# A first product that streams 512 columns instead of 448 in the half-size block products

## The chip, the cores and the metric

One NeuronCore of a Trainium2 chip runs the whole kernel. The metric is the device time of one execution in microseconds (us); several runs are taken and their median is compared. One execution is also recorded by the hardware profiler, and all rows below come from that record.

## The reference

The reference is attention followed by two feed-forward blocks, all in float32.

```
scores = cap * tanh(scale * q @ k.T / cap)          # 2 batches x 12 heads, 448 x 448, head size 64
x = softmax(scores) @ v  -> (896 tokens, 768)
x = x / sqrt(mean(x*x) + 1e-6) * rms_g              # first block
x = (silu(x @ w_gate) * (x @ w_val)) @ w_out        # 768 -> 1536 -> 768
h = x @ w_in                                        # second block, 768 -> 2048
out = (max(h, 0) + alpha * min(h, 0)) @ w_out       # 2048 -> 768
```

## The kernel before, in words

Tokens lie along the free dimension: each of the two batches has S = 448 tokens, so every large matmul streams 448 columns. A float32 number is split into a high part and a low part of the type fp32r, and a product of two such numbers is made from three matmuls: high by high, low by high and high by low.

The program has four stretches after attention, written out by hand in one order for all engines (`manual_schedule`). Stretch g is the first layer of the first block, o its second layer, z the first layer of the second block, f its second layer. The first layers g and z multiply 2 x 2 blocks in a scheme with seven half-size products (P1 to P7) instead of eight; the sums and differences that this takes are made by VectorE (`tt`, L564), and weights are combined on GpSimd (L115). The second layers o and f are plain sums over the inner dimension (L657, L659 and L661).

One half-size product is `product` (L373): for each of two rows r (two halves `ps[:, r, :]` of a PSUM pair of banks) nine matmuls (L380) add into the same 448 columns: three inner blocks k (K3 = 3) times the three high/low pairs. So a product is 18 matmuls, and each has its own weights, which TensorE loads ahead of it (LDWEIGHTS, PEld in the profile). A bank holds 512 columns, of which 448 are used; every reader takes `[:, :, :S]`. The moving operand `xh` is a tile of 128 x 3 x 448, so its three blocks k lie behind each other.

`slots` is the list of products in program order. `pslot` (L613) makes a slot of g or z; around the slots, `do` hangs the work of the other engines (weight splitting `w_hi` L120 and `w_lo` L124, evacuations L515 and L564, activations L894 and L897). The weight units come by DMA (L93), three at a time. TensorE runs the slots in the written order; a matmul waits when its weights' split (ScalarE, VectorE), its operand or its PSUM bank is not ready.

`pslot` calls `product` for 62 slots: 34 in g and 28 in z. Four more products of g stand outside it (the calls in the prologue, before 128 us), and P5 and P6 of the first two groups of g go through another function (`products`, L385).

Of the kernel before, what the change touches and what calls it, by code (L numbers as in the profile page):

```python
# [18 lines left out]
B, H, S, D = 2, 12, 448, 64  # L19
# [17 lines left out]
K3 = KD // 2  # L37
# [17 lines left out]
def attn_moe_kernel(ctx: ExitStack, tc: tile.TileContext, units, qk_in, v, sel, w, gvec, alpha, cap, out):  # L55
# [314 lines left out]

    fill_ps = {}

    def product(ps, u, name, first, rows=(0, 1)):  # L373

        wh, wl = h_t[u], l_t[u]
        xh, xl = oper[name]
        for r in rows:
            mm = [(a[:, r * K3 + k, :], x[:, k, :]) for a, x in ((wh, xh), (wl, xh), (wh, xl)) for k in range(K3)]
            for n, (lhs, rhs) in enumerate(mm):
                nc.tensor.matmul(  # L380
                    ps[:, r, :S], lhs, rhs, start=first and n == 0, stop=n == len(mm) - 1,
                    skip_group_check=True,
                )

    def products(pss, us, name):  # L385

        xh, xl = oper[name]
        both = [(ps, u) for ps, u in zip(pss, us)]
        mm = [(p, x, k, m) for k in range(K3) for p, x in ((h_t, xh), (l_t, xh)) for m in both]
        mm += [(h_t, xl, k, m) for m in both for k in range(K3)]  # L390
        for n, (wt, x, k, (ps, u)) in enumerate(mm):
            for r in range(2):
                nc.tensor.matmul(  # L393
                    ps[:, r, :S], wt[u][:, r * K3 + k, :], x[:, k, :], start=n < len(both),
                    stop=x is xl and k == K3 - 1, skip_group_check=True,
                )


    with tc.manual_schedule():
# [25 lines left out]
        r = raw.pop(0)  # L425
# [95 lines left out]
        norm_now(last)  # L521
        late = []
        product(pa[0], ("g", 0, "A11"), "B11", True, rows=(0,))
        norm(last - 1, "u")
        square(last - 1)
        product(pa[0], ("g", 0, "A11"), "B11", True, rows=(1,))
        for m in range(NP - 3, NP):
            xnorm(m, late)
# [6 lines left out]
        sum4("g", 1)  # L535
        rms_tail(B - 1)
        product(pa[1], ("g", 1, "A11"), "B11", True)
        first_sum(1, ct("c21"))
        w_hi(("g", 1, "S1"))
# [13 lines left out]
        def psum():  # L553
            turn[0] += 1
            return pair_tile(*pools[(turn[0] - 1) % 4])
# [55 lines left out]
        BANK = {"P1": pa, "P2": pa, "P6": pb, "P7": pb, "P4": pb, "P5": pc, "P3": pc}  # L611

        def pslot(lay, p, g):  # L613

            first = p in ("P1", "P6", "P5")
            wn, xn = OPER[p]

            def pe():
                if first:
                    BANK[p][g] = psum()  # L620
                if lay == "g" and p in ("P5", "P6") and g < 2:
                    if g == 1:
                        products([BANK[p][0], BANK[p][1]], [("g", i, wn) for i in range(2)], xn)
                    return
                product(BANK[p][g], (lay, g, wn), xn, first)

            at_of[lay, g, p] = len(slots)
            slots.append((pe, (lay, g, wn)))
# [409 lines left out]
```

## Time and profile before

| | us |
|---|---|
| median of 3 runs | 587.43 |
| the three runs | 584.61, 587.43, 587.48 |
| the profiled execution, its own time | 588.38 |
| the profiled execution, span from first to last instruction | 586.6 |

The stretches of the profiled execution, by the lines of TensorE: attention and the prologue to 143.5 us, products of g by `pslot` from 143.5 to 270.6 (612 matmuls), o to 359.9 (432), z to 465.4 (504), f to the end (576). In the rows, a matmul's own duration (some 367 ns) is longer than the time from one start to the next (some 205 ns), since matmuls are pipelined; the time from start to start is what counts here and is called the gap.

### The profile page before, as it was taken

The numbers are of one execution on the slowest core, as the hardware profiler recorded it, in microseconds if no ns is written. First come the engines' busy times: TensorE is split into PE (matmuls) and PEld (weight loads), VectorE is DVE, ScalarE is ACT, GpSimd is POOL, SyncE is SP. The second block draws the span as 40 slices with busy tenths as digits, with TensorE's granted clock in tenths as the row PEclk, the third lists the DMA queues.
The fourth block names the chain that finished last, engine by engine and source line by source line (L and its number), as shares of the span: only waits on it lengthen the run. The fifth ranks groups of instructions, "written<-read, shape, count | busy, mean of one in ns | idle before, by whom it ended". The sixth has DMA issues, their size and how long they took to land.

```text
span 586.6 us, 7330 instructions
## 1 busy us (share of the span) xinstructions
PE 576.8 (98%) x2939; PEld 475.1 (81%) x2939; DVE 391.8 (67%) x425; ACT 342.4 (58%) x393; POOL 111.1 (19%) x60
## 2 busy tenths in 40 slices
PE   8999999999999999999999999999899999999997
PEld 5444434598899999999999999999899989999996
DVE  5557997999997577669642563879976977613100
ACT  6999979668454453465724344577765986332101
POOL 0002873110056144110000072402441000000000
PEclk9999999999999999999999999999999999999999
DMA  8655420310234444023651633005421435431002
GB/s 272 210 195 168 132 76 20 117 46 1 95 122 161 117 152 162 7 101 108 215 162 57 237 137 108 0 1 162 139 78 57 138 129 162 161 149 55 0 1 94
DMA packets 16650, 66.05 MB, mean 113 GB/s; under 512 B 3560, under 2 KB 4200, under 8 KB 16616
## 3 DMA queue, kind: packets, MB, share of 16 engines
q1 hardware_dynamic: 16040, 65.07, 33.3%
q8 instruction: 23, 0.38, 0.3%
q10 hardware_dynamic: 432, 0.38, 0.2%
q0 software_dynamic: 144, 0.13, 0.1%
q14 instruction: 11, 0.09, 0.0%
HBM read 62.66 MB, written 2.75 MB: 112 GB/s over the span
## 4 chain that ended last, share of the span: by engine, by line
PE 81%; DVE 9%; ACT 5%; issue 2%; DMA 2%; SPq 0%; ACTq 0%; DVEq 0%
PE s L380 19%; PE m L380 14%; PE m L661 6%; PE m L659 6%; PE m L657 6%; PE oo L212 5%; PE s L659 5%; PE s L661 5%; PE s L657 5%; PE s L189 4%; DVE b L564 2%; PE us L228 2%; DVE wt L107 2%; PE m L393 1%; DVE wl L124 1%
## 5 line engine op out<-in xcount | busy, mean ns | idle before, releaser
L124 DVE TENSOR_TENSOR wl<-wt,wh 128x768 fp32r<-128x768 f32 x98 | 105.9, 1088 | 93.3 <-ACT wh L120 93.0
L115 POOL TENSOR_TENSOR wt<-wt 128x768 f32<-128x768 f32 x40 | 91.5, 2295 | 260.3 <-DVE wt L107 146.4
L120 ACT CAST wh<-wt 128x768 fp32r<-128x768 f32 x98 | 81.4, 835 | 87.3 <-PE m L659 37.2
L103 ACT CAST top<-raw 128x768 f16<-128x768 bf16 x68 | 72.6, 1075 | 47.3 <-DVE wt L107 39.3
L107 DVE SCALAR_TENSOR_TENSOR wt<-raw,top 128x768 uint32<-128x768 uint32 x68 | 69.5, 1025 | 3.5 <-ACT top L103 3.4
L380 PE MATMUL s<-xh,wh 128*128 128x448 f32 x222 | 58.2, 370 | 0.0
L380 PE MATMUL s<-xl,wh 128*128 128x448 f32 x222 | 57.7, 368 | 0.0
L380 PE MATMUL s<-xh,wl 128*128 128x448 f32 x222 | 57.7, 368 | 0.0
L661 PE MATMUL m<-ks,wl 128*128 128x448 f32 x176 | 51.6, 367 | 0.0
L657 PE MATMUL m<-ks,wh 128*128 128x448 f32 x176 | 51.6, 367 | 0.0
L380 PE MATMUL m<-xh,wh 128*128 128x448 f32 x174 | 45.5, 369 | 1.8 <-ACT b L515 1.5
L661 PE MATMUL s<-ks,wl 128*128 128x448 f32 x160 | 47.0, 366 | 0.0
L657 PE MATMUL s<-ks,wh 128*128 128x448 f32 x160 | 46.9, 366 | 0.0
L380 PEld LDWEIGHTS s<-xh,wh 128*128 128x128 f32 x222 | 41.5, 188 | 5.5 <-issue 0.9
L199 ACT ACTIVATE pt<-s,cinv 128x896 f32<-128x896 f32 (+1 forms) x48 | 41.3, 908 | 7.6 <-PE s L189 7.4
L659 PE MATMUL m<-b,wh 128*128 128x448 f32 x156 | 45.6, 367 | 0.0
L380 PE MATMUL m<-xh,wl 128*128 128x448 f32 x174 | 45.2, 368 | 0.0
L380 PE MATMUL m<-xl,wh 128*128 128x448 f32 x174 | 45.2, 367 | 0.0
L380 PEld LDWEIGHTS s<-xl,wh 128*128 128x128 f32 x222 | 41.7, 188 | 4.1
L380 PEld LDWEIGHTS s<-xh,wl 128*128 128x128 f32 x222 | 41.7, 188 | 4.0
L212 PE MATMUL oo<-pt,vt 128*64 128x448 f32 x192 | 41.3, 551 | 1.0 <-ACT pt L201 1.0
L201 ACT ACTIVATE pt<-pt,cap_t 128x1792 f32<-128x1792 f32 (+1 forms) x24 | 38.6, 1607 | 0.8
(143 smaller groups left out, 909.8 us busy)
## 6 DMA issues: line engine op xcount, KB each, us to landing
raw<-w_in SPq DMA_DIRECT2D x68, 768.0 KB
rw<-qk_in SPq DMA_DIRECT2D x11, 480.0 KB
vt<-v_in SPq DMA_DIRECT2D x12, 256.0 KB
out<-o SPq DMA_DIRECT2D x5, 448.0 KB
gt<-us SPq DMA_DIRECT2D x22, 3.5 KB
rw<-qk_in ACTq DMA_DIRECT2D x1, 256.0 KB
rw<-qk_in SPq DMA_DIRECT2D x1, 224.0 KB
out<-o SPq DMA_DIRECT2D x1, 224.0 KB
```

The lines of the kernel that those rows point to most:

```text
L103: nc.scalar.copy(top_of[u].bitcast(F16)[:, 1::2], raw_t[u].bitcast(BF16)[:, 4:4 * UW + 4:4])
L107: nc.vector.scalar_tensor_tensor(out=f_t[u].bitcast(U32), in0=raw_t.pop(u).bitcast(U32)[:, 1:2 * UW + 1:2], scalar=13, in1=top_of.pop(u), ...
L115: nc.gpsimd.tensor_tensor(out=t, in0=f_t[a], in1=f_t[b], op=op)
L120: nc.scalar.copy(h_t[u], f_t[u].rearrange("p (k m) -> p k m", m=P))
L124: nc.vector.tensor_tensor(out=l_t[u], in0=f_t[u].rearrange("p (k m) -> p k m", m=P), in1=h_t[u], op=ALU.subtract)
L199: nc.scalar.activation(out=t[:, n:n + w], in_=st.pop((i, g))[:, :w, :S], func=AF.Tanh, scale=cinv)
L201: nc.scalar.activation(out=t[:, :n], in_=t[:, :n], func=AF.Exp, scale=cap_t)
L212: nc.tensor.matmul(oo[i][h * D:h * D + D, :S], vv[:, 2 * c + h, :], t[:, n, :], start=c == 0, stop=c == 3, skip_group_check=True,)
L380: nc.tensor.matmul(ps[:, r, :S], lhs, rhs, start=first and n == 0, stop=n == len(mm) - 1, skip_group_check=True,)
L657: nc.tensor.matmul(dst[l], wh[:, o, :], xh[l], start=first, stop=False)
L659: nc.tensor.matmul(dst[l], wh[:, o, :], xl[l], start=False, stop=False)
L661: nc.tensor.matmul(dst[l], wl[:, o, :], xh[l], start=False, stop=fin)
```

## The change

`product` gets a flag `wide`, which `pslot` sets. With it the first matmul of row 0 (high by high, k = 0) streams 512 columns of the flattened operand: the 448 of block k = 0 and the first 64 of block k = 1. Its output is 512 columns of the bank, of which columns 448 to 511 are read by nobody. All other matmuls are as before.

```
-    def product(ps, u, name, first, rows=(0, 1)):
+    def product(ps, u, name, first, rows=(0, 1), wide=False):
         wh, wl = h_t[u], l_t[u]
         xh, xl = oper[name]
         for r in rows:
             mm = [(a[:, r * K3 + k, :], x[:, k, :]) for a, x in ((wh, xh), (wl, xh), (wh, xl)) for k in range(K3)]
+            if wide and r == 0:
+                mm[0] = wh[:, r * K3, :], xh.rearrange("p k s -> p (k s)")[:, :512]
             for n, (lhs, rhs) in enumerate(mm):
                 nc.tensor.matmul(
-                    ps[:, r, :S], lhs, rhs, start=first and n == 0, stop=n == len(mm) - 1,
+                    ps[:, r, :rhs.shape[-1]], lhs, rhs, start=first and n == 0, stop=n == len(mm) - 1,
                     skip_group_check=True,
                 )
...
-                product(BANK[p][g], (lay, g, wn), xn, first)
+                product(BANK[p][g], (lay, g, wn), xn, first, wide=True)
```

The instructions of TensorE around the first such product (P7 of group 0 of g, at 143.5 us in the trace), before; `s` and `m` are the two pools of PSUM pairs, `xh` and `xl` the operand's parts, `wh` and `wl` the weights':

```order
L393 MATMUL s<-xl,wh 128x448 x12
L380 MATMUL s<-xh,wh 128x448 x3
L380 MATMUL s<-xh,wl 128x448 x3
L380 MATMUL s<-xl,wh 128x448 x3
L380 MATMUL s<-xh,wh 128x448 x3
L380 MATMUL s<-xh,wl 128x448 x3
```

The same place in the changed kernel:

```order
L395 MATMUL s<-xl,wh 128x448 x12
L382 MATMUL s<-xh,wh 128x512
L382 MATMUL s<-xh,wh 128x448 x2
L382 MATMUL s<-xl,wh 128x448 x3
L382 MATMUL s<-xh,wh 128x448 x3
L382 MATMUL s<-xh,wl 128x448 x3
```

One matmul of the 18 is longer; nothing has moved. In all, TensorE has the same 2,939 matmuls, 62 of them with 512 columns, and the other engines have what they had.

The start of the product that stands at 192.5 us of the trace before, with the semaphores that instructions wait for, first before and then in the changed kernel:

```order
L380 MATMUL m<-xl,wh 128x448 x3
L380 MATMUL m<-xh,wh 128x448 [waits Activation_49]
L380 MATMUL m<-xh,wh 128x448 x2
```

```order
L382 MATMUL m<-xl,wh 128x448 x3
L382 MATMUL m<-xh,wh 128x512 [waits PE_49,Activation_49]
L382 MATMUL m<-xh,wh 128x448 x2
```

Here, and at the starts of two further products of g (218.5 and 244.5 us of the trace before), the wide matmul also waits for a semaphore of TensorE itself; no other wait is new.

## Rows read from the trace of the kernel before

**Rows 1.** The page: span, busy time of the engines, granted TensorE clock in 40 slices.

```profile
span 586.6 us, 7330 instructions
PE 576.8 (98%) x2939; PEld 475.1 (81%) x2939; DVE 391.8 (67%) x425; ACT 342.4 (58%) x393; POOL 111.1 (19%) x60
...
PEclk9999999999999999999999999999999999999999
```

**Rows 2.** TensorE's waits, longest first: engine, line, releaser: us, times, longest.

```profile
PE m L380 <- ACT b L515: 1.5, 1, 1.5
...
PE m L380 <- DVE c L564: 0.3, 1, 0.3
...
PE s L659 <- DVE b L564: 0.2, 1, 0.2
```

**Rows 3.** The chain that ended last, in order of time: start us, us, what.

```profile
136.05 6.21 PE s L393 x30
151.32 7.81 PE m L380 x36
159.13 7.44 PE s L380 x36
...
367.45 7.44 PE m L380 x36
374.89 18.61 PE s L380 x90
416.01 4.30 DMA raw<-w_in
424.39 3.91 PE m L380 x18
...
435.75 11.16 PE m L380 x54
446.91 3.73 PE s L380 x18
461.64 2.17 DVE ks L564 x2
```

**Rows 4.** The same chain followed back from 430 us: how it leaves TensorE.

```profile
399.51 1.09 DVE b L564
400.61 0.87 DVE wl L124
...
423.45 0.89 ACT b L515
```

**Rows 5.** Equal stretches: us, busy us of PE, PEld, DVE, ACT, POOL (x instructions), PEclk, DMA share, GB/s.

```profile
156.00:256.00 100.00, 100.00 (x486) 90.83 (x485) 74.67 (x80) 48.21 (x62) 36.75 (x16) 1.00 0.37 120
482.00:582.00 100.00, 100.00 (x495) 92.70 (x494) 31.07 (x32) 29.38 (x33) 0.00 (x0) 1.00 0.24 82
401.00:421.00 20.00, 20.00 (x100) 18.54 (x100) 20.00 (x19) 16.29 (x23) 6.97 (x3) 1.00 0.45 145
360.00:380.00 20.00, 20.00 (x99) 18.16 (x98) 16.81 (x12) 12.35 (x14) 6.20 (x2) 1.00 0.00 0
```

**Rows 6.** The chain after 480 us; 33 rows of two matmuls from 481.65 to 495.03.

```profile
480.98 0.67 PE s L659 x2
481.65 0.41 PE s L661 x2
...
495.03 0.41 PE m L661 x2
```

**Rows 7.** Order of time at a restart: start us, us, engine, line, operation, [idle before].

```profile
155.15 0.50 PEld L380 LDWEIGHTS m<-xh,wh 128*128 128x128 f32 x3 [0.32 <-issue]
...
155.66 0.60 PEld L380 LDWEIGHTS m<-xh,wl 128*128 128x128 f32 x3
```

**Rows 8.** Order of time at the restart of 400.7 us.

```profile
400.72 0.50 PEld L380 LDWEIGHTS m<-xh,wh 128*128 128x128 f32 x3 [0.18 <-issue]
```

**Rows 9.** Groups by line: weight loads of 128, 64 and 32 columns; mean ns of one.

```profile
L380 PEld LDWEIGHTS s<-xh,wh 128*128 128x128 f32 x222 | 41.5, 188 | 5.5 <-issue 0.9 <-ACT wh L120 0.4 <-PE ms L332 0.2
...
L212 PEld LDWEIGHTS oo<-pt,vt 128*64 128x64 f32 x192 | 11.7, 136 | 19.6 <-issue 16.4 <-ACT pt L201 2.4 <-ACT pt L199 0.5
...
L228 PEld LDWEIGHTS us<-pt,ones 128*32 128x32 f32 x132 | 4.3, 108 | 13.2 <-issue 8.9 <-DVE wt L107 2.8 <-DVE lo L176 0.7
```

**Rows 10.** The chain at the full float32 matmuls of the prologue.

```profile
115.20 2.25 PE ms L332 x6
```

More of the change, by code (lines that the diff above doesn't have):

```diff
@@ L371, in attn_moe_kernel, with product @@
     fill_ps = {}
-    def product(ps, u, name, first, rows=(0, 1)):
+    def product(ps, u, name, first, rows=(0, 1), wide=False):
         wh, wl = h_t[u], l_t[u]
@@ L378, in product @@
             mm = [(a[:, r * K3 + k, :], x[:, k, :]) for a, x in ((wh, xh), (wl, xh), (wh, xl)) for k in range(K3)]
+            if wide and r == 0:
+                mm[0] = wh[:, r * K3, :], xh.rearrange("p k s -> p (k s)")[:, :512]
             for n, (lhs, rhs) in enumerate(mm):
                 nc.tensor.matmul(
-                    ps[:, r, :S], lhs, rhs, start=first and n == 0, stop=n == len(mm) - 1,
+                    ps[:, r, :rhs.shape[-1]], lhs, rhs, start=first and n == 0, stop=n == len(mm) - 1,
                     skip_group_check=True,
@@ L624, in pe @@
                     return
-                product(BANK[p][g], (lay, g, wn), xn, first)
+                product(BANK[p][g], (lay, g, wn), xn, first, wide=True)
             at_of[lay, g, p] = len(slots)
```

## The prediction

> **What bounds the kernel now.** I read the page first. TensorE (PE) is busy 98% of the span, VectorE 67%, ScalarE 58%, and the granted clock is 1.00 in every slice, so 2.4 GHz of its two levels throughout [rows 1]: the clock is not in play. The waits of TensorE come next, because a change inside its stream costs nothing where it waits anyway. In g, z and f they are few: one of 1.5 us and two of 0.2 to 0.3 us [rows 2]. The chain in order of time then shows where TensorE itself sets the end. It does from 151.3 us through g and o into z [rows 3]. At 399.5 us the chain leaves it for VectorE and ScalarE and comes back only at 424.39 us [rows 4]; it leaves again at about 450.6 us (446.91 + 3.73) and comes back at 480.98 us, from where it is matmuls [rows 3, 6]. Before 151.3 us, from 142.3 us (136.05 + 6.21), it is off TensorE as well [rows 3].
>
> The last thing to see is the gap from matmul to matmul, because nearly all matmuls here have the same 448 columns, yet not the same gap. In a slow stretch 90 of them take 18.61 us, 206.8 ns each, and 36 take 7.44 us, 206.7 [rows 3]. In f, 66 take 495.03 - 481.65 = 13.38 us, 202.7 ns each [rows 6]. Two equal windows of 100 us say the same, 486 matmuls against 495, and two of 20 us, 99 against 100 [rows 5]. So there are two paces 4.0 ns apart. Neither goes with DMA traffic: the slow one stands at a DMA share of 0.37 and of 0.00, the fast one at 0.45 and 0.24 [rows 5]. The pace changes where TensorE restarts after a pause: after that of 155.15 us it is slow [rows 7] up to the next pause at 400.7 us, from which it is fast [rows 8, 5]. Between pauses it stays, over slot and layer boundaries.
>
> **The change part by part.** 62 matmuls get 64 more columns; none is added, and nothing moves on any engine.
>
> *The columns.* At one column per clock of 2.4 GHz 64 columns are 26.7 ns. Whether all of that is paid depends on what the other 20 ns of a gap are: 448 columns are 186.7 ns, the gap 206.7. If they belong to the matmul's stream (its start, or the weight load that disturbs it), the wide gap is 206.7 + 26.7 = 233.4. If instead the gap is set by the weight load and the columns hide behind it, 512 columns need at least 213.3 ns, and the wide gap grows by only some 7. Rows nearest to this: the load's record grows with its columns, 108, 136 and 188 ns for 32, 64 and 128 [rows 9], that is by 0.83 ns a column, so 128 columns are some 107 ns of loading and the rest a constant. After a pause, three loads end 0.50 us after the first began, in the stream 0.60 [rows 7]: the second load begins 0.1 us earlier than in a running stream, so the array took in the first set in about 0.11 us. That is well under 187. Full float32 matmuls with such loads run at 2.25 / 6 = 375 ns for 448 columns [rows 10], twice 187 and 2 more: a stream at half the rate hides the load altogether. Both rows speak for the load being a disturbance of a stream at full rate and not its limit, so I take 26.7 ns; the lower end is 7.
>
> The Trainium skill bears on this in "TensorE: Matmul & The Clock Gate", section "Back-to-back issue gap": an isolated warm matmul takes N / 2.4 + 2.5 ns, while a stream of load and matmul pairs is set by both. By that formula 448 columns would take 189.2 ns and 512 columns 215.8; the trace has 206.7 or 202.7 for 448, so the formula lacks a part that these pairs pay. If that part were a floor, the page's 215.8 would make each wide matmul dearer by 9.1 ns, an estimate from the page, and the sum below 0.5 us instead of 1.3.
>
> *Where it is paid.* A product of 18 matmuls takes 3.72 us [rows 3]. Of the 62 wide matmuls two stand at 143.5 and 147.3 us, before TensorE holds the chain; six lie between 399.6 and 424.3 us, and four at 450.5 us and later, where VectorE and ScalarE hold it [rows 3, 4]. There the later end of a product goes into a pause that is there already; without that cover the twelve would cost 12 x 26.7 = 0.32 us more. The 50 others are on the chain: **50 x 26.7 ns = +1.33 us** (at 7 ns: +0.35).
>
> *The new waits.* Three wide matmuls of g wait for TensorE's own semaphore. Such waits stand in z before too, at 367.3, 371.0 and 439.3 us, and the chain runs through them as unbroken PE pieces [rows 3], so they cost nothing. If one did have to wait for the matmul just ahead, it would pay at most that matmul's rest, 0.37 us of duration less 0.21 of gap, and a restart of 0.1: 0.26 each, 0.8 for three.
>
> *The pace.* This is the unknown. Nothing in the trace is a matmul longer than its neighbours inside a stream, so I bound it. On the chain and slow are the matmuls from 155.7 to 399.5 us (243.8 us / 206.7 ns = 1,180) and from 428.3 to 450.6 (some 108). If the longer matmul frees the stream from the slow pace for good, 1,288 x 4.0 ns = 5.2 us are won. If it leaves the pace as it is, nothing. If it drives a fast stretch into the slow pace, what can be lost on the chain is f: of its 576 matmuls some 75 lie before 481 us (15.6 us at 206.7 ns), the other 500 lose 2.0 us, for the pace of f comes from the restart at 480.98 us.
>
> I take no change of pace, for this reason. Both paces are steady to the nanosecond, so they look like a lock to some fixed beat. 206.67 ns is 31 x 6.67; five fast gaps, 1,013.3 ns, are 152 x 6.67; and 64 columns at 2.4 GHz, 26.67 ns, are 4 x 6.67. A matmul that lasts exactly four beats longer would leave the next one at the same place in the beat, slow or fast as it was. This is an inference from gaps, not something that a row shows.
>
> **Sum.** The profiled execution took 588.38 us, 0.95 above the median of 587.43 and close to two of the three runs; with +1.33 it would be 589.7. Against the median: 587.43 + 1.33 = **588.8 us**. The three runs lie 2.9 us apart; a run with a fast pace after 155 us would be some 4.8 us (1,180 x 4.0) shorter than one without, so part of that scatter may be this very thing. About 0.5%, 2.9 us, is what a measurement of this kernel can tell from no change.
>
> **The rivals.**
> *The slow pace breaks (faster).* For it: the pace does change at disturbances, and each product would now begin with one, 62 in all; at a restart as small as the one of 400.7 us, idle 0.18 us, it went from slow to fast [rows 8]. If the wide gap is not a whole number of beats (the floor case gives 213 to 216 ns, which is none), each wide matmul is a new throw. Against it: the four beats above. Price: -5.2 + 1.3 = -3.9, so 583.5 us; with the cheap columns 582.6. If the throws fall evenly to both paces, about half of the 5.2 is won: 587.43 - 2.6 + 1.0 = 585.8.
>
> *The columns are nearly free (no change).* The weight load is the floor, the pace stays: +0.35, 587.8. For it only that the load's record, 188 ns, is close to 187; against it the 0.11 us after a pause and the float32 row.
>
> *The slow pace spreads to f (slower).* Its place is the restart at 480.98 us, which VectorE releases [rows 6, 2]. Every time before it shifts with the longer products, and so does the point at which the stream sets off. If it sets off slow, f costs 2.0 us more: 587.43 + 1.33 + 2.0 = 590.8, slower by 0.57%. It decides as soon as more than 390 of the 500 matmuls are slow. For it: the restart at 155.15 us led into the slow pace [rows 7]; against it: those of 400.7 and 480.98 us led into the fast one.
>
> **How the numbers follow.** Forecast, no change of pace: 0.42. Slow pace broken for most of the way: 0.29. Even throws: 0.10. Columns nearly free: 0.06. Slow f: 0.13. Faster by over 0.5% (under 584.5) takes most of the broken pace (0.25), a fifth of the even throws (0.02) and a twentieth for a forecast in which the restart of 155 us falls fast by itself (0.05): 0.32. Slower (over 590.4) takes most of slow f (0.10) and an eighth of the forecast, for scatter of the runs (0.05): 0.15. The rest, 0.53, is within 0.5%. The likeliest case alone reaches from 587.4 to 590.4; the range for 8 in 10 goes from 582.8, which takes in the broken pace, to 590.9, which takes in slow f.
>
> **What would show it.** A wide matmul's gap: 233 ns supports the forecast, 213 to 216 the floor. The chain's rows of a product, x18: 3.72 + 0.03 = 3.75 us in g means slow and paid; 3.65 + 0.03 = 3.68 means the pace broke. The windows of 100 us in g and o: 486 matmuls less three or four for the wide ones, or 495. The o stretch has no wide matmul and 432 equal ones: 89.3 us if slow, 87.6 if fast; it is the cleanest sign. The restart at 480.98 us and the count in a 100 us window behind it tell the third rival. The prediction is wrong if o runs at 202.7 ns after the change, or if f runs at 206.7.

## The result and the profile after

The changed kernel took 589.69 us (median of 11 runs, 588.1 to 592.24), the kernel before in the same session 584.61 us (median of 11, 582.73 to 587.48): 1.0085 times as long, 95% interval 1.0057 to 1.0113. It is slower, beyond the 0.5% that I had set as the bound. Two later sessions gave 1.003 (0.9991 to 1.0069) and 1.0086 (1.0054 to 1.0118). The runs of the kernel before do not scatter evenly but stand in groups some 2 to 3 us apart. The three runs and the profile that the prediction started from were mostly from an upper group of the kernel before, and that matters below.

The page of the profiled execution (591.67 us by its own time), with the rows that answer to [rows 1]:

```profile
span 589.9 us, 7333 instructions
PE 579.3 (98%) x2939; PEld 475.1 (81%) x2939; DVE 391.6 (66%) x425; ACT 341.9 (58%) x393; POOL 111.2 (19%) x60
PEclk7999999999999999999999999999999999999999
```

TensorE has 2.5 us more busy time; no other engine's busy time has moved by more than 0.5 us. In this one execution the clock was granted late, in the first of the 40 slices (0.83 over the first 20 us). The chain at the start waits for a DMA as well. The same DMA stands there in four of the later profiles, with 4.7 to 5.4 us, and nowhere as long as here:

```profile
1.18 5.94 DMA cap_t<-cap_in
```

The first products of g by `pslot` begin 144.8 us after the first matmul in place of 142.5; so 2.3 us of this execution are a matter of its start, and I leave them out of what follows. The chain from there, in order of time, beside [rows 3]:

```profile
161.45 7.48 PE s L382 x36
168.93 7.48 PE m L382 x36
...
377.89 18.71 PE s L382 x90
...
427.64 3.95 PE m L382 x18
431.59 7.41 PE s L382 x36
439.00 11.22 PE m L382 x54
450.22 3.75 PE s L382 x18
464.96 2.17 DVE ks L566 x2
```

A product of 18 matmuls takes 3.74 us where it took 3.72 (7.48 / 2; 18.71 / 5 beside 18.61 / 5). That is the slow pace plus 20 ns, so the longer matmul did not break the pace. One product in the order of time, TensorE alone:

```profile
191.00 0.37 PE L382 MATMUL s<-xl,wh 128*128 128x448 f32 x1
191.21 0.81 PE L382 MATMUL m<-xh,wh 128*128 128x512 f32 x3
191.85 0.78 PE L382 MATMUL m<-xh,wl 128*128 128x448 f32 x3
192.47 0.78 PE L382 MATMUL m<-xl,wh 128*128 128x448 f32 x3
193.09 0.78 PE L382 MATMUL m<-xh,wh 128*128 128x448 f32 x3
```

From 191.21 to 191.85 us are three gaps, 0.64 us in place of 0.62. Read one by one from the trace, the gap behind the wide matmul is 235 ns; then come 205, 205 and 201, and from the fifth on 206.7 again on average. The stream pays 28 ns for the 64 columns and takes some 8 of them back in the next three gaps.

In z there is a fast stretch between two pauses, as before. Here the wide matmul does something else:

```profile
411.28 0.80 PE L382 MATMUL s<-xh,wh 128*128 128x512 f32 x3
411.91 0.77 PE L382 MATMUL s<-xh,wl 128*128 128x448 f32 x3
412.52 0.77 PE L382 MATMUL s<-xl,wh 128*128 128x448 f32 x3
413.13 0.77 PE L382 MATMUL s<-xh,wh 128*128 128x448 f32 x3
413.74 0.77 PE L382 MATMUL s<-xh,wl 128*128 128x448 f32 x3
414.35 0.77 PE L382 MATMUL s<-xl,wh 128*128 128x448 f32 x3
414.95 0.80 PE L382 MATMUL m<-xh,wh 128*128 128x512 f32 x3
415.59 0.78 PE L382 MATMUL m<-xh,wl 128*128 128x448 f32 x3
```

The product of 411.28 us is fast: three matmuls in 0.61 us. That of 414.95 us begins in the fast pace and goes on at 0.62 (415.59 to 416.21). No pause lies between. A wide matmul has led the stream from the fast pace into the slow one, and the same happens at 435.1 us.

### The profile page after: what moved, and what is told of

Its sections match the earlier page's. It is cut to its first block, busy times and chain, and to the rows that moved or that the text cites. A ratio compares the mean times of both kernels' runs of the same rounds, so it can differ in the third digit from the quotient of the medians.

```text
span 589.9 us, 7333 instructions
## 1 busy us (share of the span) xinstructions
PE 579.3 (98%) x2939; PEld 475.1 (81%) x2939; DVE 391.6 (66%) x425; ACT 341.9 (58%) x393; POOL 111.2 (19%) x60
## 4 chain that ended last, share of the span: by engine, by line
PE 81%; DVE 9%; ACT 5%; issue 3%; DMA 2%; ACTq 0%; DVEq 0%; SPq 0%
PE s L382 19%; PE m L382 14%; PE m L663 6%; PE m L661 6%; PE m L659 6%; PE oo L212 5%; PE s L661 5%; PE s L663 5%; PE s L659 5%; PE s L189 4%; DVE b L566 2%; PE us L228 2%; DVE wt L107 2%; PE m L395 1%; DVE wl L124 1%
## 5 line engine op out<-in xcount | busy, mean ns | idle before, releaser
L382 PE MATMUL s<-xh,wh 128*128 128x448 f32 (+1 forms) x222 | 59.1, 374 | 0.0
L382 PE MATMUL m<-xh,wh 128*128 128x512 f32 (+1 forms) x174 | 46.3, 374 | 1.5 <-ACT b L517 1.3
L212 PE MATMUL oo<-pt,vt 128*64 128x448 f32 x192 | 42.9, 569 | 0.5 <-ACT pt L201 0.5
```

The source lines that it names most:

```text
L212: nc.tensor.matmul(oo[i][h * D:h * D + D, :S], vv[:, 2 * c + h, :], t[:, n, :], start=c == 0, stop=c == 3, skip_group_check=True,)
L382: nc.tensor.matmul(ps[:, r, :rhs.shape[-1]], lhs, rhs, start=first and n == 0, stop=n == len(mm) - 1, skip_group_check=True,)
```

## The experiments

For each kernel the first question is the pace of g, o and f. Windows of 80 us answer it: some 389 matmuls mean the slow pace (386 or 387 where wide ones are among them), some 396 the fast one. For the changed kernel, in g, o and f (us, PE busy (x matmuls), and so on as in [rows 5]):

```profile
180.00:260.00 80.00, 80.00 (x387) 72.27 (x386) 54.32 (x59) 37.54 (x47) 27.37 (x13) 1.00 0.34 114
275.00:355.00 80.00, 80.00 (x389) 72.66 (x388) 43.85 (x43) 32.76 (x36) 10.86 (x5) 1.00 0.46 156
490.00:570.00 80.00, 80.00 (x397) 74.15 (x396) 26.65 (x27) 22.61 (x25) 0.00 (x0) 1.00 0.27 93
```

The o stretch, which has no wide matmul, is slow (389), as in [rows 3] of before; f is fast.

**The kernel before once more.** No edit.

> The kernel before, unchanged, for another profile of it. Theory A (the pace is thrown at the restart near 155 us and then kept): the runs fall into two groups some 3 to 5 us apart, and this profile is near 583.5 us if its o stretch holds 432 matmuls in 87.6 us (202.7 ns each) and near 587.4 us if it takes 89.3 us (206.7 ns each). Rival B (the scatter of the runs comes from the start, where a DMA lands late): o takes 89.3 us in a run of either group.

Ten runs, median 584.78 us (582.14 to 587.91). The profiled one took 584.81 us:

```profile
180.00:260.00 80.00, 80.00 (x396) 74.16 (x395) 56.46 (x61) 40.32 (x50) 25.96 (x12) 1.00 0.33 111
275.00:355.00 80.00, 80.00 (x397) 74.15 (x396) 40.29 (x38) 34.72 (x38) 14.21 (x6) 1.00 0.48 168
490.00:570.00 80.00, 80.00 (x389) 72.66 (x388) 20.30 (x21) 17.79 (x21) 0.00 (x0) 1.00 0.21 75
```

The same program, unchanged, runs g and o fast here and f slow: the opposite of the profile that the prediction was made from. In its chain 90 matmuls take

```profile
370.06 18.25 PE s L380 x90
```

and o takes 87.55 us in place of 89.28 (first start to the first start behind it, from the trace). So the pace can differ from one execution to the next, for g with o and for f apart. With 4.7 us for g and o and 2.0 us for f, the prediction's own terms, that makes four groups: near 582.8 (both fast), 584.9 (f slow), 587.5 (g and o slow) and 589.8 us (both slow). The runs stand at these times. Of the kernel before only two executions have a profile, this one and the first, so which group a run without a profile belongs to is inferred from its time. Rival B falls as the main cause. Of the 97 runs of the kernel before that were measured beside the others, 58 were under 586 us: 6 of 11, 14 of 31, 19 of 31 and 19 of 24 in the four sets. The ten runs here, of the same program, come on top, 8 of them under 586 us beside the 14 of 31 of their own session; so the shares scatter too.

**Other widths: 456, 464 and 480 columns.** The changed kernel with another number in one line, in all 62 products:

```
-                mm[0] = wh[:, r * K3, :], xh.rearrange("p k s -> p (k s)")[:, :512]
+                mm[0] = wh[:, r * K3, :], xh.rearrange("p k s -> p (k s)")[:, :456]
```

> The 62 first matmuls stream 456 columns: 8 more, 3.3 ns, half of a beat of 6.67 ns. Theory A (a beat of 6.67 ns; only whole beats leave the slow pace in place): the slow pace breaks, a product of 18 matmuls in g takes 3.65 us, o takes 87.6 us, total 582 to 584 us. Rival B (any longer first matmul leaves the stream slow, since slow is where it falls back to): product 3.72 us plus at most 0.01, o 89.3 us, total 587 to 589 us.

> 464 columns: 16 more, 6.7 ns, one whole beat. Theory A (whole beats leave the pace as it is): a slow g stays slow, product 3.727 us, o 89.3 us if g was slow; a fast g stays fast. Rival B (falls back to slow): product 3.72 to 3.73 us, o 89.3 us, total 588 us, the same as with 456.

> 480 columns: 32 more, 13.3 ns, two whole beats; half of the columns of the change. Theory A: as with 464, the pace of g as its restart threw it, each product 13 ns longer. Rival B: product 3.727 us, o 89.3 us, total some 588 us.

| columns | median us (runs) | ratio to before of its session, 95% | gap behind the wide matmul from the slow pace | the product then |
|---|---|---|---|---|
| 456 | 588.16 (10) | 1.0046 (1.0015 to 1.0076) | 211 ns | slow, 56 of 56 |
| 464 | 585.62 (10) | 0.9987 (0.9956 to 1.0019) | 214 ns | fast, 14 of 14 |
| 480 | 586.63 (10) | 1.0012 (0.998 to 1.0044) | 221 ns | fast, 19 of 19 |
| 512, the change | 589.69 (11) | 1.0085 (1.0057 to 1.0113) | 235 ns | slow, 51 of 51 |

The last row is of the first session, the others of one later session. The last two columns are counted in the one profile of each, over the wide matmuls that come behind four gaps of 206 or 207 ns and have no pause in their own gap. Both theories fall: 8 columns did not free the stream (against A), and 16 and 32 did (against A and B). With 464, g shows a pattern in its chain, followed back from 200 us:

```profile
165.38 7.32 PE m L382 x36
172.70 3.72 PE s L382 x18
176.42 3.66 PE m L382 x18
180.08 7.37 PE s L382 x36
187.45 7.31 PE m L382 x36
194.76 3.72 PE s L382 x18
```

Two fast products (7.32 / 2 = 3.66 us), one slow (3.72), over and over. In the trace of single gaps the fast pace is a cycle of five, 199, 207, 202, 203 and 202 ns. With 464 and 480 columns the wide matmuls that lead out of it stand behind gaps of 202 and 203, where the gap of 199 would come next (35 of 35); at the other places that the profiles show it goes on. From the slow pace each wide matmul behind four such gaps leads back; one of 480 columns with a gap of 204 ns just ahead of it did not. So what a longer matmul does depends on its length and on the place in the cycle at which it falls. I call this theory A3; the expectations that follow were written with its coarser forms, under the name A2.

**The change again.** No edit.

> The changed kernel once more, for a second profile. Theory A2 (512 columns lead into the slow pace and never out of it): g and o slow in this profile too, a product of g 3.74 us, o 89.3 us; no run under 587.5 us. Rival C (the change only costs its columns, and the pace of g and o is thrown as before): o takes 87.6 us in about half of the profiles, and runs near 584.5 us turn up.

Ten runs, median 587.51 us (584.92 to 590.84), 1.003 (0.9991 to 1.0069). The profile has g and o slow (387 and 389 in the two windows), as A2 wants. But five of the ten runs are under 587.5 us, two of them by a wide margin, 584.92 and 585.29, so "no run under 587.5" fails and "never out of it" is too strong. The same profile shows how: in z, from 428 us on, ten products with 512 columns in a row stay fast, each wide matmul at the same place of the cycle. A fast stream can keep its pace under the change if it happens to meet that place.

**512 columns in z alone.**

```
+        def KICK(lay, g, p):
+            return (0, 0, 512) if lay == "z" else None
...
-                product(BANK[p][g], (lay, g, wn), xn, first, wide=True)
+                product(BANK[p][g], (lay, g, wn), xn, first, wide=KICK(lay, g, p))
```

The three numbers are the row, the place among its nine matmuls and the columns; `product` takes them in place of the flag.

> 512 columns in the 28 products of z alone. Theory A2: g and o are thrown as in the kernel before, so the runs spread as those do; only z is forced slow: over the kernel before it is 19 x 20 ns = 0.4 us of columns on the chain and up to 0.8 us (some 200 matmuls x 4 ns) where z was fast, median some 0.5 to 1 us above before. Rival D (each wide matmul costs the same, whatever the pace): 28/62 of the change's loss, 1.5 to 2.3 us above before, and the fast group of runs near 583 us is gone.

Ten runs, median 586.11 us (582.79 to 590.19), 1.002 (0.9985 to 1.0055). The fast group is there (582.79, 583.19, 583.84), which speaks against D. In the profile, g and o are fast (396 and 396) and z is slow in 22 of 28 products. The median is 1.3 us above that of before, between the two theories' sizes, and inside the spread of before, so it tests neither. What the profile does show is the fall itself. The stream has been fast through g and o, and the first wide matmul of z leaves it so; the second leads it into the slow pace, with no pause near:

```profile
355.68 0.80 PE L384 MATMUL s<-xh,wh 128*128 128x512 f32 x3
356.31 0.77 PE L384 MATMUL s<-xh,wl 128*128 128x448 f32 x3
356.92 0.77 PE L384 MATMUL s<-xl,wh 128*128 128x448 f32 x3
...
359.35 0.80 PE L384 MATMUL s<-xh,wh 128*128 128x512 f32 x3
359.99 0.78 PE L384 MATMUL s<-xh,wl 128*128 128x448 f32 x3
360.61 0.78 PE L384 MATMUL s<-xl,wh 128*128 128x448 f32 x3
```

The gap just ahead of the first is 207 ns, that ahead of the second 199. This holds throughout. The three profiles of the change, this one and the one with 464 in the last product of g (below) have 50 matmuls of 512 columns in a settled fast cycle: 12 stand directly behind the gap of 199 (once 200), and all 12 lead into the slow pace; 38 stand elsewhere, and all 38 leave the stream fast. From one product to the next the place moves. Counted in gaps since the last 199, it goes from 3 to 4, from 4 to 1, from 1 to 0, and 0 is the fall; only from 2 it comes back to 2. So of five places four end in the slow pace within four products, and one keeps the fast pace, as the ten products above did.

**One matmul of 512 columns.** As above, for P4 of group 0 in g alone.

```
+            return {("g", 0, "P4"): (0, 0, 512)}.get((lay, g, p))
```

> One matmul of 512 columns in the whole kernel (the first of P4 of group 0 in g, near 159 us). Theory A2: from the slow pace it stays slow; from the fast one it falls to slow in some places of the cycle of five, so at most some of the runs of the fast group are lost: median between that of before and 1.5 us above it. Rival D: no change to within 0.05 us.

Ten runs, median 587.76 us, 1.0036 (1.0002 to 1.0071); nine of the ten between 587.27 and 589.24, one at 582.7. The median is 2.95 us above that of before (31 runs, 19 of them under 586 us), against D and more than I had expected. But that one matmul caused the loss is not shown. In its profile the stream was slow already ahead of it (from the restart near 151 us) and stayed so. In the two profiles that have g fast and no wide matmul there, this matmul starts one gap after the 199 (158.3 us, the kernel before once more) and four gaps after it (158.7 us, 512 in z alone), where 512 columns kept the pace in every case counted above. Whether the other eight runs were led into the slow pace by this matmul, or were thrown so, their times cannot say.

**Seven matmuls of 464 columns, meant to lead out of the slow pace.** Two in g, two in z, three in f (the first of f begins the sum over the same 464 columns of the bank to which the later two add); all others as before.

```
+            return {("g", 2, "P1"): (0, 0, 464), ("g", 2, "P6"): (1, 0, 464),
+                    ("z", 3, "P1"): (0, 0, 464), ("z", 3, "P6"): (1, 0, 464)}.get((lay, g, p))
...
+                    if (name, half, u, o) in (("f", 0, 0, 0), ("f", 0, 3, 0)):
+                        dst[0], xh[0] = banks[m][:, 0, :464], kwide[name, u // 2][at_[0]]
...
+                    if (name, half, u, o) == ("f", 0, 4, 0):
+                        dst[0], xh[0] = banks[m][:, 0, :464], kwide[name, u // 2][at_[0]]
```

> Seven matmuls of 464 columns in the whole kernel, all other 448: two in g (P1 and P6 of group 2), two in z (P1 and P6 of group 3), three in f (its first, and the first two of the fourth and fifth units that can read on). Theory A2 (464 columns out of the slow pace lead into the fast one, and a second one at another place of the cycle of five mends the case in which the first led out of the fast one): o 87.6 us, f fast behind the fourth unit, all runs in one group near 582 to 584 us, faster than both kernels by 0.4 to 1%. Rival B (slow is where a stream falls back to): runs spread as those of before, median within 0.3% of it.

> The kernel with seven matmuls of 464 columns again. Theory A3: one group of runs at 582.9 to 584 us, o 87.6 us, 0.3% under the median of before and 0.7% or so under that of the change. If the first time was chance, two groups as before.

The first time 583.1 us, all ten runs between 582.91 and 583.93, 0.9968 of before (0.9939 to 0.9996); the second time 583.29 us, twelve runs between 583.04 and 584.16, 0.9971 (0.9944 to 0.9998). The medians alone would not decide, for that of before in the second of these sessions is 583.45 us, 0.16 above; the spread does: it has shrunk from some 7 us to 1.3, and the slower groups are gone. The moment in g, followed back from 190 us in the chain of the first:

```profile
158.80 7.44 PE s L384 x36
166.24 7.31 PE m L384 x36
173.55 3.65 PE s L384 x18
```

The products up to 166.2 us are slow; the one that begins with 464 columns there, and all behind it, are fast. In o and f:

```profile
275.00:355.00 80.00, 80.00 (x397) 74.13 (x396) 40.74 (x38) 34.70 (x38) 14.20 (x6) 1.00 0.49 168
490.00:570.00 80.00, 80.00 (x397) 74.12 (x396) 20.30 (x21) 18.57 (x21) 0.00 (x0) 1.00 0.22 76
```

In the second profile the first of the two in z led out of the fast pace (427.35 us), and the other back into it (436.65 us), which is the case that the pair was meant for. This version is faster than the change by 1.0% where their medians are of one session (583.29 against 588.97 us), and than the kernel before by 0.3% by the ratios, whose intervals end just under 1.

**The change with 464 in the last product of g.**

```
-                product(BANK[p][g], (lay, g, wn), xn, first, wide=True)
+                product(BANK[p][g], (lay, g, wn), xn, first, wide=464 if (lay, g, p) == ("g", G1 - 1, "P3") else 512)
```

> The changed kernel, but the first matmul of the last product of g (P3 of group 5) streams 464 columns instead of 512. Theory A3 (a pace is a place in a beat; from the slow one 464 columns lead out, 512 do not): g as in the change, slow at 3.74 us a product in most runs, but o fast, 87.6 us in place of 89.3, so about 1.7 us under the change where that was slow. Rival D (o is slow because of what runs beside it, or the change costs its columns alone): o 89.3 us, the same time as the change to 0.1 us.

> The changed kernel a third time, for its spread beside the kick. Theory A3: between 585 us (g and o by chance fast, with their columns) and 592 us, in groups, with no run under 584 us; median 1 to 5 us above before. Rival C (columns alone): the same two groups as before, each 1.3 us later.

In its profile g is slow and o fast, 387 and 396 matmuls:

```profile
180.00:260.00 80.00, 80.00 (x387) 72.28 (x386) 53.60 (x59) 37.94 (x48) 25.96 (x12) 1.00 0.31 102
275.00:355.00 80.00, 80.00 (x396) 74.13 (x396) 42.78 (x40) 33.79 (x37) 14.19 (x6) 1.00 0.48 163
```

One number in one matmul takes 1.73 us off o (87.55 against 89.28 us), and it is the last matmul group ahead of it, not what runs beside o, that decides. In time: 587.31 us (twelve runs, 586.47 to 588.83) beside 588.97 for the change itself (seven runs, 588.32 to 590.8), 1.66 us less. The change's third set (588.97 us, 1.0086 of before) stays above 588 us in every run, while 19 of the 24 runs of before beside it are under 586 us. That is 5.5 us between the medians, a little beyond the 1 to 5 expected. In its profile g, o and f are slow. The two runs near 585 us in the second set were what C asked for; over the three sets they are 2 of 28, and C is out.

## Why the prediction was right or wrong

The time, 589.69 us, lies in the range, near its upper end, and 0.9 us from the forecast. The direction was not the likeliest: I gave no change the chance 0.53 and slower 0.15, and it is slower by 0.85%. The nearness of the time is luck in large part: it was built on a base of 587.43 us that eight further runs brought down to 584.61, and the 1.33 us that I added stood against a measured 5.08.

**The columns.** I took 26.7 ns for each wide matmul and 50 of them on the chain, 1.33 us. The gap itself grew by 28 ns (235 against 206.7), so the floor rival, 213 to 216 ns, is out, and the reading of the weight loads [rows 9, 10] held. A product in the slow pace grew by only 20 ns, since the next three gaps are shorter: 50 x 20 ns = 1.0 us. The term was mis-sized by a quarter. The number 50 is one or two too high as well: the chain of before leaves TensorE at 393.50 us (374.89 + 18.61 in [rows 3]), not at 399.5; that is under 0.06 us.

**The new waits** cost nothing: the three products with a new wait on TensorE's own semaphore lie inside the unbroken stretch of equal products from 161.45 us.

**The step that failed** is "I take no change of pace", with its reason that 64 columns are four whole beats. For the slow pace the conclusion held, 51 of 51 products stayed slow. The reason did not: one and two whole beats (464 and 480 columns) led out of the slow pace each time, and half a beat (456) did not. And for the fast pace the conclusion failed: 512 columns led from fast to slow at two points of the profile after, and in all five profiles with such matmuls in a fast stretch each time that one fell directly behind the gap of 199 ns (12 of 12). I had seen the opposite kind of risk, that f might be thrown slow, and priced it. A fast g stood in my sums only as a gain, with a chance of 0.05, and I had no case in which g and o were fast to begin with and the change took that away. The profile that I read had them slow, so nothing there could be lost, and I took that for the kernel's nature, although the three runs already lay 2.9 us apart and I had said what might lie behind it.

**Where the 5 us come from.** Over all sessions the mean of before is 585.61 us (97 runs) and of the change 589.08 (28 runs), 3.5 us apart. 58 of the 97 runs lie under 586 us, where by the groups above g and o are fast; of the 28, two to five do (two under 586, three more between 586.5 and 586.8 which could be fast in g and o with a slow f). By the prediction's own term, 1,180 matmuls of 4.0 ns are 4.7 us for a run in which g and o turn from fast to slow; a share of 0.42 to 0.53 more runs is 2.0 to 2.5 us. With the columns' 1.0 us that is 3.0 to 3.5, an estimate. The share fits the five places: if fast starts met them evenly, which no run shows, one in five of some 0.6 would stay fast, 3 of 28 runs. One step is argued and not seen: in all three profiles of the change g was slow from its restart near 155 us on, so the fall of a fast g is seen only in its first products (146.6 us in the second profile) and otherwise in z. The larger figure of the first session has in it which throws fell in it; its eleven runs cannot be split further without a profile of each.

**The rivals.** The broken slow pace did not come with 512 columns but was real: with 464 at the right places it gave 583.1 and 583.29 us, where I had written 583.5, though with seven longer matmuls and not with 62. The slow f happens (the third profile of the change has 389 matmuls in the window of f), but also in the kernel before, so it isn't shown to be the change's doing. By the signs that I had named, the first profile bore the prediction out, with o in 89.28 us and f fast; the third, with f slow, did not.

**Open:** what the beat is. The trace gives its places and what each length does at them, not which part of the chip keeps it. With 512 columns all five places were met, one of them (3) only once; with 464 and 480 columns not all were. What throws the pace at a pause, and why nine of ten runs with a single matmul of 512 columns were slow, is not settled.

## What to carry to other kernels

Where nearly all matmuls are alike, look at the gap from start to start and not at the busy share: two paces 2% apart hide behind the same 98%. If runs of one kernel stand in groups, one profile is one throw; compare the profile's own time with several runs, and take a second profile before a sum is made against the first. A pace that is thrown at pauses can be set by hand with a few matmuls of another length, but the length and the place have to be measured: 16 more columns and 64 more columns did opposite things.

## What the hardware showed that I had not expected

- fp32r matmuls of 448 columns, each with its own weights, run back to back at 206.7 ns or in a cycle of five that averages 202.7 ns, at a granted clock of 1.00. Each pace held for over 400 matmuls, and in these profiles it changed only at a pause or at a matmul of another length. A delay as small as one gap of 229 ns among equal matmuls was pause enough (the kernel before, 428.13 us, directly behind a gap of 199): from there the stream was slow.
- From the slow pace a matmul of 456 or 512 columns returns to it within four or five matmuls; one of 464 or 480 columns ends in the fast pace. From the fast pace, 512 columns led into the slow one directly behind the gap of 199 ns (12 of 12) and nowhere else (0 of 38); 464 and 480 columns did so where that gap would have come next (36 of 36).
- The gap of a 512-column matmul was 235 ns from the slow pace and 226 to 236 ns from the fast one, by its place in the cycle.
